# The low part of layer one's activations: made by VectorE in every step instead of by GpSimd in the first 75

## The chip, the cores and the metric

The kernel runs on one core of a Trainium2 chip. The metric is the time of one execution on the device in microseconds (us); lower is better. The core's engines run in parallel, each from its own queue, in order: PE (TensorE, matmuls), DVE (VectorE), ACT (ScalarE), POOL (GpSimd) and SP (SyncE, which here issues every DMA).

## The reference: Nystrom attention and two dense layers

```python
x = attn_out.transpose(...).reshape(2304, 512)      # Nystrom attention, 4 batches of 8 heads
h = x @ w_in                                        # layer one: 512 -> 2048
g = h * (1 / (1 + exp(-h)))
x = g @ w_out                                       # 2048 -> 512
h = x @ w_in2                                       # layer two, the same sizes
out = (h * tanh(log1p(exp(h)))) @ w_out2
```

All arrays are float32. The activation of layer one, g, is what the change touches.

## The kernel before, in words

Every product that must be exact is computed from split operands: a value x is kept as a high part (x rounded to the matmul's format) and a low part (x minus the high part), and a product is three matmuls, high times high, high times low and low times high (`mm3`, line 639 in the profile).

The program has three stretches. A prologue (to about 180 us) computes the attention of batches 0 and 1, converts the first layer's weights and does the first two blocks of layer one; its order on all engines is written out by a planner with costs. Then comes the loop this change is in: 96 steps `t`, each for one block of 288 tokens and one of 16 slices of the hidden layer. At the end (from about 470 us) layer two runs, in an order written by hand.

A step of the loop does the following. PE computes `h(t)` with six matmuls into one of two PSUM banks (`bank((4, 6)[t % 2])`), so the bank of step t is used again by step t+2. `silu2` then makes the activation in a chain of four instructions, each on the result of the one before: ACT takes the tanh (L698), DVE multiplies (L699; this is the last reader of the PSUM bank), ACT casts the result to the high part (L700), and one engine subtracts to get the low part (L701). PE then consumes both parts in the twelve matmuls of `y(t)`, which are issued two steps later (`LAG = 2`: `emit_y(t - LAG)`). The second of the twelve already needs the low part.

Other work is dealt out between the steps:

- `advance` issues the attention of batches 2 and 3: softmax pieces on POOL (L501, L509, L526), many small DVE instructions, and the Newton iterations, where PE (L441) and DVE (L445, L453) wait for each other in turn.
- `cv2` converts the weights of layer two. Each of its 32 pieces is loaded into one of three buffers by a DMA, clamped by POOL (L621), scaled twice by ACT (L623, L624) and put together by DVE (L626, L630).
- `u_all` makes the next batch's left operands.

In the first 75 steps (`t < AHEAD`) no order is prescribed: the framework orders each engine's instructions itself, by when its own model finds them ready, with earlier program text first. So instructions that stand side by side in the text (L626 and L630) can lie apart in the trace. From step 75 on, the order on ACT, DVE, PE and POOL is that of the program text (`manual_schedule`).

Of the kernel before, what the change touches and what calls it, by code (L numbers as in the profile page):

```python
# [25 lines left out]
AHEAD = 75  # L26
# [65 lines left out]
def nystrom_moe_kernel(ctx, tc, q, k, v, w1i, w1o, w2i, w2o, out):  # L92
# [10 lines left out]
    act, dve, pool, pe, sp = nc.scalar, nc.vector, nc.gpsimd, nc.tensor, nc.sync  # L103
# [38 lines left out]
    def bank(i, name):  # L142
        return ps.tile([P, 512], F32, tag=f"b{i}", name=name)
# [438 lines left out]
    def u_all(b, jq):  # L582
        for _ in u_steps(b, (2 * jq, 2 * jq + 1)):
            pass
# [86 lines left out]
    def h1_matmuls(hb, b, j, hf):  # L671
        uh, ul = uq[b, j // 4][:, 0], uq[b, j // 4][:, 1]
        sl = slice(hf * HB, (hf + 1) * HB)
        for g in range(2):
            wh, wl = uh[:, g, j % 4], ul[:, g, j % 4]
            xh, xl = ath[b][:, g, sl], atl[b][:, g, sl]
            mm3(hb[:, :HB], [(wh, xh), (wh, xl), (wl, xh)], g == 0, g == 1)
# [16 lines left out]
    def silu2(hb, gh, gl, name, eng=dve):  # L694

        th = mp.tile([P, HB], F32, tag="th", name="th" + name)
        g2 = mp.tile([P, HB], F32, tag="g2", name="g2" + name)
        tanhs.append(act.activation(th, hb[:, :HB], AF.Tanh, scale=0.5))  # L698
        dve.scalar_tensor_tensor(g2, th, 1.0, hb[:, :HB], op0=ALU.add, op1=ALU.mult)  # L699
        act.copy(gh, g2)  # L700
        eng.tensor_tensor(gl, g2, gh.bitcast(F32), op=ALU.subtract)  # L701
# [32 lines left out]
    def advance(n=1.0):  # L734
        credit[0] += n
        while credit[0] >= 1:
            credit[0] -= 1
            while bg:
                try:
                    next(bg[0])  # L740
                    break
                except StopIteration:
                    bg.pop(0)
# [9 lines left out]
    def attn_batch(b):  # L753
        if b == 2:
            yield Step((), [("wt", 1, 1), ("ath", 1, 1)] + [("ci", j) for j in OWN])
        for g in range(2):
            units[b, g] = new_unit(b, g)
            yield from whole_unit(units[b, g], True)
            if g == 1:
                yield from attn_newton(batches[b][g])  # L760
# [158 lines left out]
    gt = {}  # L919
# [21 lines left out]
    def open_second():  # L941
        rgt.close()
        late["pool"] = ctx.enter_context(tc.tile_pool(name="p2", bufs=1, side="right"))
# [78 lines left out]
    def left_steps(n):  # L1022

        if n >= NP:
            yield from left_loads(n)
            return
        f = Left(n)
        yield
        f.sums("s1", "s2", "s4")
        f.parts(1, 6)  # L1030
        yield
        f.sums("s3")
        f.parts(2, 7)
        yield
        f.parts(5, 4)
        yield
        f.parts(3)
        yield
# [36 lines left out]
    def out_weights(js, tile_of):  # L1075

        raws = []
        for n, j in enumerate(js):
            raw = tile_of(n)
            if is64:  # L1080
                sp.dma_start(raw, w2c[NF + j])
            else:
                sp.dma_start(raw.rearrange("p (a n) -> p a n", a=1), wout_src(w2o, j))
            raws.append(raw)
        yield
        for j, raw in zip(js, raws):
            hi, lo = wout_high(2, j), half(2, j)
            split(raw, hi, lo, pool)
            wout2[j] = (hi, lo)
            yield  # L1090

    def gtiles(t, n):
        gt_ = wp.tile([P, 2, n], F32R, tag=f"gt{t % 3}", name=f"g{t}_{n}")
        return gt_[:, 0], gt_[:, 1]

    def emit_y(t):
        i, j = steps1[t]
        if j == 0:
            ybank[i] = [bank(m, f"y{i}_{m}") for m in range(ND)]
        y_matmuls(ybank[i], wout[j], *gt.pop(("a", t)), j == 0, j == NF - 1)  # L1100
        if j == NF - 1:
            y_out(ybank[i], i)
# [3 lines left out]
    for t in range(len(steps)):  # L1106
        i, j = steps[t]
        b, hf = i // 2, i % 2
        if hf == 1 and b + 1 < B and j == SHIFT + 1:
            while bg:  # L1110
                advance()
            if b + 2 < B:
                bg.append(attn_batch(b + 2))
        if t == AHEAD:
            for _ in cv2:
                pass
            open_second()
            wx = [wp.tile([P, 768], F32, tag=f"wc{c}", name=f"x0_{c}") for c in (4, 5, 6)]
            xx = [xp.tile([P, 768], F32, tag=t, name=f"x0_{t}") for t in ("ath0", "atl0")]
            xx += [lambda: wp.tile([P, 768], F32, tag="wl7", name="x0_wl")]  # L1120
            r0, l0 = Right(0, wx + xx), Left(0, dve)
            ls, wsteps = [], []

            def raw_pair(j):
                tile_ = wp.tile([P, 2, 512], F32, tag="wc7", name=f"wr{j}")
                wsteps.append(out_weights((j, j + 1), lambda n: tile_[:, n]))
                next(wsteps[-1])

            plan = {
                2: lambda: r0.sum(1),  # L1130
                3: lambda: (r0.sum(3), r0.put(1, dve)),
                4: lambda: (r0.sum(2), l0.sums("s1")),
                5: lambda: (l0.sums("s2"), r0.put(6, dve)),
                6: lambda: (l0.sums("s4"), r0.put(7, dve), raw_pair(0)),
                7: lambda: (l0.sums("s3"), r0.put(2, dve)),
                8: lambda: r0.sum(4),
                9: lambda: (l0.parts(1), r0.put(5, dve), next(wsteps[0])),
                10: lambda: (l0.parts(6), r0.put(4, dve), next(wsteps[0])),
                11: lambda: (l0.parts(2), r0.put(3, dve)),
                12: lambda: (l0.parts(7, 5), raw_pair(2)),  # L1140
                13: lambda: (l0.parts(4, 3), ls.append(Left(1))),
                14: lambda: next(wsteps[1]),
                15: lambda: next(wsteps[1]),
                16: lambda: (ls[0].sums("s1", "s2"), ls.append(left_steps(2)), next(ls[1])),
                17: lambda: (ls[0].sums("s4"), ls[0].parts(1, 6)),
                18: lambda: (ls[0].sums("s3"), ls[0].parts(2, 5)),
                19: lambda: ls[0].parts(7, 4),
                20: lambda: ls[0].parts(3),
            }
            turn = ExitStack()  # L1150
            turn.enter_context(tc.manual_schedule(engines={act.engine, dve.engine, pe.engine, pool.engine}))
        hb = bank((4, 6)[t % 2], f"h{t}")
        h1_matmuls(hb, b, j, hf)
        gt["a", t] = gtiles(t, HB)
        silu2(hb, *gt["a", t], f"{t}", pool if t < AHEAD else dve)
        lin = NF * hf + j - NF - 1 - SHIFT
        if lin >= 0 and lin % 4 == 0 and b + 1 < B:
            u_all(b + 1, lin // 4)
        lin += 2 * NF
        if b > 1 and lin < NF and lin % 4 == 0:  # L1160
            u_all(b, lin // 4)
        advance(RB)
        if t < AHEAD:
            while cvn[0] < min(34, (18 * (t - 11) // 52 if t < 64 else t - 45)):
                cvn[0] += 1
                next(cv2, None)
        if t >= LAG:
            emit_y(t - LAG)
        if t >= AHEAD and t - AHEAD in plan:
            plan[t - AHEAD]()  # L1170
        advance(RB)
# [234 lines left out]
```

## Time and profile before

| | us |
|---|---|
| median of three runs | 850.02 (849.99 to 851.71) |
| the profiled execution | 849.09 |
| its span, first to last instruction | 847.3 |
| PE busy over the span | 816.8 (96%) |
| DVE busy | 518.3 (61%) |
| ACT busy | 349.4 (41%) |
| POOL busy | 213.8 (25%) |

The spans of the instructions are from the hardware profiler. A wait is the idle time of an engine in front of an instruction, put down to what released it. "PEld" is the weight load that runs ahead of each matmul. A clock of 1.00 is TensorE's full level, 0.50 its half level.

### The profile page before, as it was taken

The page shows a single profiled execution, that of the slowest core. Times are in us where ns is not written, and L with a number is a line of the kernel's source. Part 1 is how long each engine was busy: PE and PEld are TensorE (multiplying, and loading weights), DVE is VectorE, ACT ScalarE, POOL GpSimd, SP SyncE. Part 2 cuts the span into 40 slices and gives each one's busy share as a digit, 9 for nine tenths or more (in the row PEclk, how much of TensorE's full clock was granted, in tenths as well). Part 3 has the DMA queues.
Part 4 walks back from the last instruction along what each step waited for, and adds up shares of the span by engine and source line. Part 5 has one row for each costly group of instructions (what it writes and reads, how often), then busy time and mean ns, then how long its engine had stood idle before and what let it go on. Part 6 is the DMA issues. An engine that isn't in the chain of part 4 may idle for free.

```text
span 847.3 us, 14581 instructions
## 1 busy us (share of the span) xinstructions
PE 816.8 (96%) x5350; PEld 718.0 (85%) x5350; DVE 518.3 (61%) x1067; ACT 349.4 (41%) x787; POOL 213.8 (25%) x256
## 2 busy tenths in 40 slices
PE   8789999999999998899999999999999999999998
PEld 6656776769999797899999989999999999899996
DVE  4878877687575868773386765656533456534433
ACT  4657655355344646664456543424211124211111
POOL 1311333015342536543113654512000002000000
PEclk9999999999999999999999999999999999999999
DMA  8735474335337455752216854445733334533301
GB/s 243 205 103 153 149 231 140 70 97 156 87 84 196 121 151 206 240 180 85 70 43 220 299 204 174 158 165 163 233 103 130 119 112 137 183 115 112 125 1 74
DMA packets 109175, 123.64 MB, mean 146 GB/s; under 512 B 54064, under 2 KB 82224, under 8 KB 109104
## 3 DMA queue, kind: packets, MB, share of 16 engines
q1 hardware_dynamic: 109104, 122.72, 46.4%
q8 instruction: 42, 0.69, 0.4%
q14 instruction: 29, 0.24, 0.1%
HBM read 90.18 MB, written 32.51 MB: 145 GB/s over the span
## 4 chain that ended last, share of the span: by engine, by line
PE 77%; DVE 8%; issue 4%; POOL 4%; ACT 3%; DMA 2%; SPq 2%; POOLq 0%; DVEq 0%; ACTq 0%
PE o L1226 23%; PE y L639 14%; PE px L1241 12%; PE py L1241 9%; PE h L639 7%; PE ha L669 4%; PE ya L872 3%; PE u L556 2%; SPq L216 1%; POOL g L701 1%; PE nw L441 1%; POOL rawt L621 1%; DMA rawo<-in_moe_w_out_dram 1%; PE cv L390 1%; DMA k<-in_k_dram 1%
## 5 line engine op out<-in xcount | busy, mean ns | idle before, releaser
L639 PE MATMUL y<-g,wh 128*128 128x288 f32 x768 | 162.3, 302 | 6.1 <-POOL g L701 3.9
L1226 PE MATMUL o<-wh,gm 128*128 128x512 f32 x576 | 166.3, 392 | 0.0
L639 PEld LDWEIGHTS y<-g,wh 128*128 128x128 f32 x768 | 124.8, 190 | 12.4 <-POOL g L701 5.3
L1226 PEld LDWEIGHTS o<-wh,gm 128*128 128x128 f32 x576 | 107.1, 188 | 16.5
L639 PE MATMUL y<-g,wl 128*128 128x288 f32 x384 | 115.0, 299 | 0.0
L1241 PE MATMUL px<-r,le 128*128 128x384 f32 x564 | 114.2, 338 | 0.1
L1241 PEld LDWEIGHTS px<-r,le 128*128 128x128 f32 x564 | 101.1, 188 | 7.6 <-ACT u L1344 0.6
L701 POOL TENSOR_TENSOR g<-g,g 128x288 fp32r<-128x288 f32 x75 | 64.7, 863 | 148.0 <-ACT g L700 114.5
L639 PE MATMUL h<-ath,uw 128*128 128x288 f32 x384 | 94.8, 301 | 1.9 <-DVE g L699 1.9
L1265 DVE TENSOR_TENSOR u<-u,py 128x384 f32<-128x384 f32 x47 | 26.0, 554 | 103.0 <-PE py L1241 102.9
L1241 PE MATMUL py<-r,le 128*128 128x384 f32 x420 | 85.2, 338 | 0.0
L1226 PE MATMUL o<-wl,gm 128*128 128x512 f32 x288 | 84.8, 389 | 0.0
L699 DVE SCALAR_TENSOR_TENSOR g<-th,h 128x288 f32<-128x288 f32 x96 | 43.1, 450 | 52.1 <-ACT th L698 47.9
L1241 PEld LDWEIGHTS py<-r,le 128*128 128x128 f32 x420 | 74.6, 188 | 0.3 <-DVE u L1265 0.3
L639 PEld LDWEIGHTS y<-g,wl 128*128 128x128 f32 x384 | 73.0, 190 | 0.4 <-issue 0.4
L639 PEld LDWEIGHTS h<-ath,uw 128*128 128x128 f32 x384 | 67.6, 190 | 5.8 <-issue 2.8
L872 PE MATMUL ya<-gs,wl 128*128 128x288 f32 x256 | 68.3, 412 | 1.1 <-DVE yo L726 0.9
L700 ACT CAST g<-g 128x288 fp32r<-128x288 f32 x96 | 41.4, 432 | 57.6 <-DVE g L699 57.4
L1226 PEld LDWEIGHTS o<-wl,gm 128*128 128x128 f32 x288 | 54.1, 188 | 11.4
L698 ACT ACTIVATE th<-h 128x288 f32<-128x288 f32 x96 | 39.3, 409 | 54.3 <-PE h L639 53.2
L872 PEld LDWEIGHTS ya<-gs,wl 128*128 128x128 f32 x256 | 46.6, 190 | 15.5 <-issue 2.6
L639 PE MATMUL h<-atl,uw 128*128 128x288 f32 x192 | 57.1, 297 | 0.0
(218 smaller groups left out, 1252.2 us busy)
## 6 DMA issues: line engine op xcount, KB each, us to landing
le<-lsc SPq DMA_DIRECT2D x48, 512.0 KB, 3.3
lsc<-le SPq DMA_DIRECT2D x24, 512.0 KB, 2.9
rawi<-in_moe_w_in_dram SPq DMA_DIRECT2D x16, 512.0 KB, 4.8
rawo<-in_moe_w_out_dram SPq DMA_DIRECT2D x16, 512.0 KB, 3.6
rawt<-in_moe_w_in_dram SPq DMA_DIRECT2D x16, 512.0 KB, 4.5
w2c<-ct SPq DMA_DIRECT2D x32, 256.0 KB, 2.4
rawt<-in_moe_w_out_dram SPq DMA_DIRECT2D x16, 512.0 KB, 4.0
v<-in_v_dram SPq DMA_DIRECT2D x32, 144.0 KB, 3.3
```

Source lines behind the costliest of these rows:

```text
L216: sp.dma_start(t[:, h2] if apart else t[:, :, h2, :], src[b, heads[h2]].rearrange("(p c) d -> p c d", c=NC))
L556: pe.matmul(ub[g][32 * h : 32 * h + 32, 2 * P * n : 2 * P * n + 2 * P].rearrange("a (j f) -> a j f", j=2), units[b, g]["wt"][sl, h], wcp[j ...
L639: pe.matmul(o, a, b_, start=first and i == 0, stop=last and i == n - 1)
L669: pe.matmul(hb[:, :HB], uq[0, j // 4][:, g, j % 4], ath[0][:, g, hf * HB : (hf + 1) * HB], start=g == 0, stop=g == 1)
L698: tanhs.append(act.activation(th, hb[:, :HB], AF.Tanh, scale=0.5))
L699: dve.scalar_tensor_tensor(g2, th, 1.0, hb[:, :HB], op0=ALU.add, op1=ALU.mult)
L700: act.copy(gh, g2)
L701: eng.tensor_tensor(gl, g2, gh.bitcast(F32), op=ALU.subtract)
L872: pe.matmul(yb[hf, m][:, :HB], wof[j][:, m * P : (m + 1) * P], gst[j // 4][:, j % 4, hf], start=j == 0, stop=j == NF - 1,)
L1226: pe.matmul(obank[ch], g[:, c * P : (c + 1) * P], w, start=p == 0 and ch not in seen, stop=end)
L1241: pe.matmul(o, x[:, dt], y[:, dt], start=first and m == 0, stop=m == 5, skip_group_check=True)
L1265: dve.tensor_tensor(o, a, b_, op=ALU.add)
```

## The change

```diff
         hb = bank((4, 6)[t % 2], f"h{t}")
         h1_matmuls(hb, b, j, hf)
         gt["a", t] = gtiles(t, HB)
-        silu2(hb, *gt["a", t], f"{t}", pool if t < AHEAD else dve)
+        silu2(hb, *gt["a", t], f"{t}", dve)
```

The last argument is the engine of L701, `eng.tensor_tensor(gl, g2, gh.bitcast(F32), op=ALU.subtract)`: 128 partitions by 288 elements, two inputs in SBUF. Of the 96 instructions, 75 change engine. Nothing else in the program text changes.

## Rows read from the trace of the kernel before

**Rows 1.** Windows: us; busy us (and instructions) per engine; clock; DMA share; GB/s.
```profile
184.00:416.00 232.00, 220.97 (x1850) 204.88 (x1847) 152.34 (x336) 119.15 (x281) 103.06 (x116) 0.99 0.50 147
180.00:200.00 20.00, 18.03 (x129) 15.46 (x129) 15.87 (x32) 11.48 (x30) 8.54 (x10) 1.00 0.61 168
200.00:220.00 20.00, 19.90 (x163) 19.48 (x163) 17.09 (x39) 10.59 (x24) 10.45 (x12) 1.00 0.47 107
...
280.00:300.00 20.00, 17.91 (x147) 16.49 (x144) 17.54 (x38) 13.40 (x33) 12.13 (x13) 0.93 0.47 138
...
320.00:340.00 20.00, 16.59 (x117) 14.61 (x116) 17.45 (x35) 12.30 (x30) 13.73 (x14) 1.00 0.58 201
...
360.00:380.00 20.00, 20.00 (x177) 18.97 (x176) 15.27 (x28) 12.49 (x29) 10.45 (x12) 1.00 0.57 192
```

**Rows 2.** Waits of PE, 184 to 416 us: waiter, releaser, total us, times, longest.
```profile
PEld y L639 <- POOL g L701: 5.3, 6, 2.3
PE nw L441 <- DVE rv L453: 2.3, 1, 2.3
```

**Rows 3.** Line 701's instructions: duration ns min/median/max, first and last start.
```profile
L701 POOL TENSOR_TENSOR g<-g,g x75: 791/807/1355, 185.5 to 413.8; 128x288 fp32r<-128x288 f32 x75
...
L701 DVE TENSOR_TENSOR g<-g,g x21: 457/459/611, 416.2 to 465.3; 128x288 fp32r<-128x288 f32 x21
```

**Rows 4.** Waits of DVE in the last 21 steps, columns as in rows 2.
```profile
DVE g L701 <- ACT g L700: 10.5, 21, 0.6
```

**Rows 5.** Timeline, 293 to 297 us: start, length, engine, line, operation [idle before].
```profile
293.23 0.43 ACT L700 CAST g<-g 128x288 fp32r<-128x288 f32 x1 [1.28 <-DVE g L699]
...
294.37 0.68 DVE L626 SCALAR_TENSOR_TENSOR rawt<-rawt 128x512 uint32<-128x512 uint32 x1
...
295.08 0.64 POOL L621 TENSOR_SCALAR rawt<-rawt 128x512 f32<-128x512 f32 x1 [2.80 <-DMA rawt<-in_moe_w_in_dram]
295.67 0.80 POOL L701 TENSOR_TENSOR g<-g,g 128x288 fp32r<-128x288 f32 x1
...
296.13 0.46 DVE L699 SCALAR_TENSOR_TENSOR g<-th,h 128x288 f32<-128x288 f32 x1 [1.07 <-ACT th L698]
...
296.52 0.40 PE L639 MATMUL y<-g,wh 128*128 128x288 f32 x1 [2.09 <-POOL g L701]
```

**Rows 6.** Windows of 2 us around two stalls of PE, columns as in rows 1.
```profile
296.00:298.00 2.00, 1.48 (x8) 1.48 (x9) 1.82 (x4) 1.71 (x5) 1.33 (x2) 0.79 0.48 151
298.00:300.00 2.00, 2.00 (x11) 1.95 (x10) 1.00 (x3) 0.75 (x2) 1.24 (x2) 0.50 0.00 0
300.00:302.00 2.00, 2.00 (x38) 1.31 (x38) 1.75 (x5) 0.56 (x2) 0.00 (x0) 0.86 0.12 19
...
334.00:336.00 2.00, 0.80 (x6) 0.54 (x5) 2.00 (x4) 0.33 (x1) 1.25 (x1) 1.00 0.85 250
```

**Rows 7.** Timeline, 350 to 354 us, columns as in rows 5.
```profile
351.15 1.08 POOL L621 TENSOR_SCALAR rawt<-rawt 128x512 f32<-128x512 f32 x1
...
352.95 0.69 DVE L626 SCALAR_TENSOR_TENSOR rawt<-rawt 128x512 uint32<-128x512 uint32 x1 [0.88 <-ACT rawt L623]
...
353.90 0.69 PE L441 MATMUL nw<-rv,rb 128*128 128x96 f32 x4 [2.30 <-DVE rv L453]
```

**Rows 8.** DVE, two lines of the weight conversion: durations, columns as in rows 3.
```profile
L626 DVE SCALAR_TENSOR_TENSOR rawt<-rawt x29: 670/694/1518, 201.5 to 375.5; 128x512 uint32<-128x512 uint32 x29
...
L630 DVE SCALAR_TENSOR_TENSOR ct<-rawt x32: 636/686/1643, 187.7 to 376.2; 128x512 uint32<-128x512 uint32 x32
```

**Rows 9.** Groups by line, 184 to 416 us: busy us, mean ns | idle before.
```profile
L701 POOL TENSOR_TENSOR g<-g,g 128x288 fp32r<-128x288 f32 x75 | 64.7, 863 | 148.0 <-ACT g L700 114.5 <-PE y L639 28.1 <-issue 4.4
...
L630 DVE SCALAR_TENSOR_TENSOR ct<-rawt 128x512 uint32<-128x512 uint32 x32 | 27.5, 861 | 0.2
L626 DVE SCALAR_TENSOR_TENSOR rawt<-rawt 128x512 uint32<-128x512 uint32 x29 | 23.6, 814 | 11.5 <-ACT rawt L623 11.2
```

**Rows 10.** Timeline near 206 us, columns as in rows 5.
```profile
205.56 0.44 DVE L699 SCALAR_TENSOR_TENSOR g<-th,h 128x288 f32<-128x288 f32 x1
...
206.41 0.29 PE L639 MATMUL h<-ath,uw 128*128 128x288 f32 x1
```

## The prediction

> **What bounds the kernel now.** I read the windows first, to see which engine is short in the stretch of the change. From 184 to 416 us, where the 75 subtractions lie on POOL, PE is busy 220.97 of 232 us at a clock of 0.99, DVE 152.34, ACT 119.15 and POOL 103.06 [rows 1]. So PE is the bound of the stretch, and only two things can move its end: PE's idle 11 us, and the little time at the lower clock. Off PE, the 20 us windows differ: DVE is busy 15.3 to 17.5 us in five of them (180, 200, 280, 320 and 360), and PE loses time in three of these. DVE's share over the whole stretch (66%) therefore says little; the five windows decide.
>
> Next come PE's waits. Weight loads of `y` waited for POOL's subtraction six times, 5.3 us in all, the longest 2.3; a single wait of the Newton matmuls for DVE cost 2.3 [rows 2]. Last I read the timelines at the longest of each kind, for what stood in the queue ahead of the late instruction [rows 5, 7].
>
> **What moves, and its cost.** POOL loses 75 instructions with a median of 807 ns, 64.7 us in all [rows 3, 9]. DVE gains 75, and the last 21 steps show the same shape there at a median of 459 ns [rows 3]: 75 x 0.459 = 34.4 us. No DMA, matmul or ACT instruction is added or taken away. What this is worth is worked out at the places where PE stands still.
>
> *First term, the six waits for POOL.* At the longest, the cast ended at 293.23 + 0.43 = 293.66. POOL's in-order queue had a weight clamp ahead of the subtraction, and the clamp waited for its DMA until 295.08; the subtraction ran at 295.67 and PE went on at 296.52 [rows 5]. On DVE no clamp stands ahead: DVE ran continuously up to and through L626 at 294.37, so the subtraction fits between two of its instructions and ends near 294.3, just when PE wanted it. PE stood from about 294.27 to 296.52, 2.25 us. But a second chain is late here: the DVE multiply that frees an h bank starts only at 296.13 and ends at 296.59, because ACT's tanh was late. PE, with eleven y matmuls at about 0.134 us and 0.5 us of transposes, would want that bank at about 296.3. So about 0.4 of the 2.25 comes back as a new wait. I take 1.8 saved. The other five waits sum to 5.3 - 2.3 = 3.0, 0.6 each. There the subtraction is 0.807 - 0.459 = 0.35 shorter, and it escapes POOL's queue but waits for whatever DVE has in hand (half of some 0.7 us, by the medians of [rows 8]). The bounds are nothing saved and 3.0; I take two thirds, 2.0. First term: 3.8 us.
>
> *Second term, the clock.* After the 2.25 us stall the granted clock drops: 0.79, 0.50 and 0.86 in the three windows from 296 to 302 [rows 6]. At the half level (1.2 of 2.4 GHz) that is 0.84 + 2.0 + 0.56 = 3.4 us, and half of the work of that time, 1.7 us, is lost. A stall that leaves PE busy 0.80 of 2 us at 334 us went by at 1.00 [rows 6]. What remains of the stall at 294 is shorter than that, so I take 1.7, with nothing as the other end.
>
> *Third term, the clamp released from behind the subtraction.* At 351.15 a clamp ran directly behind a late subtraction in POOL's queue. The ACT scaling behind it made DVE wait 0.88 us in front of L626; L626 stood ahead of the Newton update L453 in DVE's queue, and PE waited 2.30 us for that [rows 7]. With no subtraction in POOL's queue the clamp goes when its data is there, and the 0.88 goes. Taken: 0.9; other end nothing, since DVE's own lateness is then what is late next.
>
> *Fourth term, what DVE gives back.* In the five dense windows DVE is idle 4.13 + 2.91 + 2.46 + 2.55 + 4.73 = 16.8 us of 100 [rows 1]. There are 75 subtractions in 232 us, so 6.5 a window: 32 x 0.459 = 14.7 us come into 16.8 us of idle. Something goes out again. L626 and L630 have medians of 694 and 686 ns but means of 814 and 861, with maxima of 1518 and 1643: (0.814 - 0.694) x 29 + (0.861 - 0.686) x 32 = 9.1 us lost, and in the timeline the long ones lie beside POOL instructions [rows 8, 9]. The subtractions are 64.7 of POOL's 103.06 us, 63%, so about 5.7 us of that loss should go with them. The load then just fits, but locally it will be late where a DVE multiply already frees its bank at the last moment: at 205.56 + 0.44 = 206.0, against PE's use of that bank at 206.41 [rows 10]. I charge one subtraction, 0.46 us, to the path in each of the five windows: 2.3 us. The bounds are nothing, and, if every added microsecond in the dense windows reached PE, 14.7.
>
> The Trainium skill (SBUF — State Buffer, section "SBUF: two separate sides") says that a DVE instruction with two SBUF inputs and a GpSimd instruction exclude each other from a shared port pair for the whole instruction. The trace agrees in size: L630's longest is 1.64 us against 0.69 [rows 8]. The rule speaks for the change where it frees L626 and L630, and against it since the subtraction itself has two SBUF inputs; the third rival weighs that.
>
> Sum: 3.8 + 1.7 + 0.9 - 2.3 = 4.1 us saved. The profiled execution took 849.09 us (its span 847.3 and 1.8 around it), so one like it should take 845.0. The median of the runs is 0.93 higher; I forecast 850.02 - 4.1 = 845.9 us. From step 75 on nothing changes, so the gain stays to the end.
>
> **Rivals.** *First: DVE held by the subtraction's own wait; slower.* In the last 21 steps DVE waits 10.5 / 21 = 0.50 us in front of each subtraction, since the cast takes that long and nothing else may pass [rows 4]. If the framework's order puts the subtraction straight behind the multiply in the first 75 too, a step costs DVE 0.46 + 0.50 = 0.96 us. In the five dense windows that is 32 x 0.96 = 30.7 us, against 16.8 of idle and 5.7 of relief: 8.2 us over, which PE waits for. In place of the fourth term's 2.3: 8.2 - 6.4 = 1.8 us slower, 851.8 us; windows of middling load add perhaps 1 or 2, so 853. It decides from a mean wait of (16.8 + 5.7 + 6.4) / 32 - 0.46 = 0.44 us on. For it: the chain of [rows 4] is the same. Against it: in the first 75 steps small DVE instructions and L626/L630 are there to go in between, and the framework orders by readiness.
>
> *Second: the gain is handed back.* The six waits go, but the multiplies and Newton updates come later by as much: fourteen of the 32 dense subtractions on the path, 14 x 0.46 = 6.4, cancel the three gains. 850.0 us. For it: PE's next waits are DVE's already [rows 2], and the order of 75 steps is drawn up afresh, so stalls can land elsewhere. Against it: 11 us of PE's idle is all there is, and DVE has 80 us of idle.
>
> *Third: the subtractions meet the rest of POOL's work.* POOL keeps 103.06 - 64.7 = 38.4 us in 41 instructions, 17% of the stretch [rows 1, 9]. Then 75 x 0.17 = 12 subtractions meet one and wait half of its 0.94 us: 5.6 us of DVE, which takes the place of the relief. If all of it reached PE: 5.6 - 4.1 = 1.5 slower, 851.5 us. Against it: the slowest subtraction on DVE so far took 611 ns where the median is 459 [rows 3].
>
> *Fourth: more comes free.* The stall of 2.3 us at the Newton step is also followed by the lower clock; if it shrinks enough, that clock loss and the rest of PE's idle go too: another 1.7 + 2, about 842 us.
>
> **How the numbers follow.** A measurement of this kernel can tell 0.2%, 1.7 us, from no change. The forecast's own range is 843 to 848 us, with a chance of 0.45; the fourth rival has 0.07, the second 0.20, the third 0.08, the first 0.20. Faster: 0.45 + 0.07 = 0.52. Within 0.2%: 0.20 + 0.08 = 0.28. Slower: 0.20. For 8 in 10 the range runs from 842 (half of the fourth rival left out) to 853 (half of the first left out).
>
> **What would show each step.** L701 stands with 96 on DVE at about 0.46 to 0.5 us, and no wait of PE for POOL's g is left (first term). The clock stays at 1.00 near 296 us (second). POOL's clamps no longer make ACT and DVE wait as long, and PE's longest Newton wait is under 2 us (third). The means of L626 and L630 fall towards 0.7 us, and PE's waits for DVE's L699 and L701 sum to 2 to 3 us (fourth). It would be wrong if DVE's idle in front of L701 comes to more than about 33 us (75 x 0.44), or if PE's waits for DVE grow by over 6 us.

## The result, and the profile after

The changed kernel takes 843.71 us (median of five runs, 841.7 to 845.28) against 850.02 for the kernel before: the ratio is 0.9911 with a 95% interval of 0.9892 to 0.9929, so 6 to 9 us are saved. A second comparison, on another chip, gave 0.9904 (0.9875 to 0.9932). The forecast was 845.9. Its direction and range hold; the gain is larger than the 4.1 us worked out, and it is made up in another way than the sum had it.

The profiled executions can be compared more sharply by stretches of the loop, each from the first h matmul of one step to that of another. Behind step 95 every profile here shows 380.5 us to the end of the last matmul, and step 0 starts anywhere between 179.7 and 186.9 us, so the loop itself is what carries the change. The second profile of the changed kernel says how far a stretch can be trusted: its loop is 1.2 us longer than the first one's. Differences under about 1.5 us are not read below.

| us | steps 0-11 | 11-33 | 33-58 | 58-75 | 75-95 | loop, 0-95 |
|---|---|---|---|---|---|---|
| before | 29.8 | 68.6 | 89.9 | 45.6 | 49.2 | 283.2 |
| changed | 28.1 | 68.6 | 83.3 | 45.7 | 49.2 | 274.9 |
| changed, second profile | 28.0 | 68.6 | 84.5 | 45.7 | 49.2 | 276.1 |

Of 8.3 us, 1.7 are gained in the first eleven steps and 6.6 in steps 33 to 58. The windows of the changed kernel answer to [rows 1], with the same columns (the loop lies about 4 us later at its start and 4 earlier at its end):

```profile
184.00:416.00 232.00, 224.64 (x1908) 208.06 (x1901) 179.96 (x420) 124.86 (x292) 39.51 (x41) 1.00 0.51 149
180.00:200.00 20.00, 18.76 (x157) 15.22 (x150) 18.20 (x38) 11.16 (x26) 3.95 (x3) 1.00 0.48 132
200.00:220.00 20.00, 20.00 (x165) 19.79 (x165) 19.33 (x51) 11.75 (x28) 3.47 (x4) 1.00 0.50 119
...
280.00:300.00 20.00, 20.00 (x173) 17.62 (x170) 18.80 (x43) 12.83 (x32) 6.09 (x6) 1.00 0.37 101
300.00:320.00 20.00, 17.63 (x163) 16.06 (x164) 15.62 (x41) 9.10 (x21) 1.78 (x3) 1.00 0.62 185
320.00:340.00 20.00, 18.47 (x138) 16.68 (x138) 18.36 (x42) 14.62 (x35) 8.83 (x9) 1.00 0.58 190
...
360.00:380.00 20.00, 19.98 (x197) 18.07 (x196) 17.18 (x35) 12.81 (x28) 3.74 (x5) 1.00 0.59 202
```

POOL falls from 103 to 40 us and DVE rises by 27.6, to 78% of the stretch and 91 to 97% of four dense windows; even so PE gains 3.7 us of busy time. PE's waits (180 to 412 us; waiter, releaser, total us, times, longest) answer to [rows 2]:

```profile
PE y L639 <- ACT g L700: 1.5, 1, 1.5
PE nw L441 <- DVE rv L453: 1.4, 1, 1.4
PE u L556 <- ACT ct L376: 1.3, 1, 1.3
PE nb L381 <- DVE uw L575: 1.1, 1, 1.1
PE h L639 <- DVE g L699: 0.7, 1, 0.7
PE nw L441 <- DVE rv L413: 0.6, 1, 0.6
PE c L323 <- DVE ta L488: 0.5, 1, 0.5
```

No wait for POOL is left, and each other one occurs once. The groups of the changed kernel on DVE answer to [rows 9] (busy us, mean ns | idle before), and behind them stand the wait that answers to [rows 4] and ACT's wait for the clamps:

```profile
L701 DVE TENSOR_TENSOR g<-g,g 128x288 fp32r<-128x288 f32 x75 | 36.8, 491 | 16.0 <-ACT g L700 15.6
...
L630 DVE SCALAR_TENSOR_TENSOR ct<-rawt 128x512 uint32<-128x512 uint32 x32 | 25.7, 803 | 0.0
L626 DVE SCALAR_TENSOR_TENSOR rawt<-rawt 128x512 uint32<-128x512 uint32 x30 | 20.7, 689 | 3.5 <-ACT rawt L623 3.1
```
```profile
DVE g L701 <- ACT g L700: 15.6, 30, 1.2
...
ACT rawt L623 <- POOL rawt L621: 2.7, 4, 1.8
```

In the kernel before (184 to 416 us) ACT's wait for the clamps was:

```profile
ACT rawt L623 <- POOL rawt L621: 13.4, 14, 1.6
```

DVE waits 15.6 / 75 = 0.21 us in front of a subtraction, not 0.50: the framework put other work in between. L626 and L630 fell by 125 and 58 ns each, together 3.6 + 1.9 = 5.5 us. L701 lost (0.491 - 0.459) x 75 = 2.4 us to what POOL still does: of the 74 subtractions that start on DVE between h of step 0 and h of step 75, the 17 that ran beside a POOL instruction took 631 ns in the mean, the other 57 took 450 and none of them more than 461.

### The profile page after: what moved, and what is told of

It reads as the page before. It is cut to its first block, busy times and chain, and to the rows that moved or that the text cites. A ratio compares the mean times of both kernels' runs of the same rounds, so it can differ in the third digit from the quotient of the medians.

```text
span 843.5 us, 14509 instructions
## 1 busy us (share of the span) xinstructions
PE 814.6 (97%) x5350; PEld 717.2 (85%) x5350; DVE 540.2 (64%) x1142; ACT 350.6 (42%) x787; POOL 150.8 (18%) x181
## 4 chain that ended last, share of the span: by engine, by line
PE 77%; DVE 10%; DMA 5%; ACT 3%; SPq 2%; issue 2%; POOL 1%; DVEq 0%; POOLq 0%; ACTq 0%
PE o L1226 23%; PE y L639 14%; PE px L1241 12%; PE py L1241 9%; PE h L639 7%; PE ha L669 4%; PE ya L872 3%; PE u L556 2%; DMA rawo<-in_moe_w_out_dram 2%; DMA q<-in_q_dram 1%; PE nw L441 1%; DMA rawt<-in_moe_w_in_dram 1%; DVE ct L630 1%; DVE wl L630 1%; SPq L205 1%
## 5 line engine op out<-in xcount | busy, mean ns | idle before, releaser
L639 PE MATMUL y<-g,wh 128*128 128x288 f32 x768 | 159.0, 299 | 2.5 <-ACT g L700 1.5
L639 PEld LDWEIGHTS y<-g,wh 128*128 128x128 f32 x768 | 123.2, 188 | 7.0 <-issue 2.5
L639 PE MATMUL y<-g,wl 128*128 128x288 f32 x384 | 113.9, 297 | 0.0
L639 PE MATMUL h<-ath,uw 128*128 128x288 f32 x384 | 93.8, 299 | 0.7 <-DVE g L699 0.7
L639 PEld LDWEIGHTS y<-g,wl 128*128 128x128 f32 x384 | 72.3, 188 | 0.8 <-issue 0.8
L639 PEld LDWEIGHTS h<-ath,uw 128*128 128x128 f32 x384 | 67.0, 188 | 4.3 <-issue 2.2
L701 DVE TENSOR_TENSOR g<-g,g 128x288 fp32r<-128x288 f32 x96 | 46.7, 487 | 26.5 <-ACT g L700 26.0
L700 ACT CAST g<-g 128x288 fp32r<-128x288 f32 x96 | 41.4, 432 | 53.3 <-DVE g L699 52.8
L699 DVE SCALAR_TENSOR_TENSOR g<-th,h 128x288 f32<-128x288 f32 x96 | 42.8, 447 | 27.1 <-ACT th L698 26.7
L639 PE MATMUL h<-atl,uw 128*128 128x288 f32 x192 | 56.9, 297 | 0.0
```

The lines of the kernel that those rows point to most:

```text
L639: pe.matmul(o, a, b_, start=first and i == 0, stop=last and i == n - 1)
```

## Experiments

Ratios are to the kernel before, in runs on the same chip, with 95% intervals. "Loop" is steps 0 to 95 as in the table above.

### Where the gain is made: steps on DVE

```diff
-        silu2(hb, *gt["a", t], f"{t}", dve)
+        silu2(hb, *gt["a", t], f"{t}", dve if t < 11 or 33 <= t < 58 or t >= AHEAD else pool)   # dense
+        silu2(hb, *gt["a", t], f"{t}", pool if t < 11 or 33 <= t < 58 else dve)                 # light
```

> The subtraction is on DVE in 36 of the first 75 steps, those of the dense windows (steps 0 to 10 and 33 to 57), and on POOL in the other 39. My theory (the gain is made where PE stood still, and those places lie in the dense windows): as the changed kernel, 843 to 845 us, and the loop from step 0 to step 95 about 275 us as there. The rival (the gain is the shorter subtraction, 0.35 us in every step): about half of it, 847 us.

> The complement: DVE in the 39 light steps (11 to 32, 58 to 74), POOL in the 36 dense ones. My theory: no gain, 849 to 851 us, and the loop about 283 us as before the change. The rival (a shorter subtraction in every step): about half of the gain, 847 us. A second rival (the gain is that the framework orders the loop anew, whatever is moved): a change of some us in either direction with stalls in other places.

Measured: the dense version has a ratio of 0.9935 (0.9912 to 0.9957) and a loop of 276.5 us; the light one 1.0003 (0.9981 to 1.0026) and 282.5. In the dense version steps 0 to 11 take 28.0 us and 33 to 58 take 84.3. So 36 of the 75 moves make nearly all of the gain, and the other 39 none that can be told (0.6 us of loop): it is not a shorter subtraction in every step, and not the fresh order as such.

### What POOL's load costs, and what DVE's costs

```diff
+        if t < AHEAD:
+            dm = mp.tile([P, HB], F32R, tag="dm", bufs=1, name=f"dm{t}")
+            pool.tensor_tensor(dm, extra[0], extra[1].bitcast(F32), op=ALU.subtract)
```

(`extra` holds g2 and gh of the step, the two inputs of L701. The second kernel has `dve.tensor_tensor` in the same place.)

> The changed kernel, with a copy of each of the 75 subtractions added on POOL whose result nobody reads. POOL is as full as before and the weight clamps stand behind the copies again, but PE waits for no POOL result. My theory (the place in POOL's queue): PE's waits for POOL's g and the clock loss after the longest of them do not come back; the clamps are held again, and DVE carries the subtractions beside a full POOL. So about half of the gain stays: 846 to 848 us. The rival (what counts is POOL's load itself, through the ports it shares with DVE): the whole gain goes and DVE's added work comes on top, 850 to 853 us. If POOL's load counts for nothing: 843 to 844.5 us.

> The changed kernel, with a copy of each of the 75 subtractions added on DVE too, whose result nobody reads: DVE gets another 34 us. DVE was idle 8.1 us in the five dense windows of the changed kernel and would get 32 x 0.46 = 14.7 there. My theory (DVE is now almost the bound of the dense windows): 6 to 9 us slower than the changed kernel, 850 to 853 us. The rival (DVE has room, PE alone is the bound): within 1.5 us of the changed kernel, 843 to 845 us.

Measured with the copies on POOL: ratio 1.0091 (1.0056 to 1.0126), loop 288.2 us. My theory fell here: PE waits for no POOL result in this kernel, and still it is slower than the one before. The rival named the mechanism and was short on the size. Measured with the copies on DVE: 0.9991 (0.9965 to 1.0016), loop 280.5 us. So a POOL copy costs the loop 288.2 - 274.9 = 13.3 us, and a DVE copy 5.6. In total the two add up to the change, 274.9 + 13.3 - 5.6 = 282.6, where the kernel before has 283.2. That is chance, for by stretches they do not. In steps 33 to 58 the POOL copies cost 8.3 us (91.6 against 83.3) and the DVE copies nothing (81.9), so the same sum would give 93.0 us there, where the kernel before takes 89.9. The DVE copies lose 2.2 us in steps 0 to 11 and 4.2 in steps 58 to 75, where they pushed five of the 19 weight conversions that the changed kernel makes in steps 33 to 58. So my theory for the DVE copies had the size nearly right, and the place, the dense windows, in part wrong. POOL's copies also run beside a DVE that subtracts, which POOL's subtractions before the change did not. The groups of the kernel with POOL copies (180 to 425 us):

```profile
L1161 POOL TENSOR_TENSOR dm<-g,g 128x288 fp32r<-128x288 f32 x75 | 73.6, 981 | 136.9 <-ACT g L700 136.8
...
L701 DVE TENSOR_TENSOR g<-g,g 128x288 fp32r<-128x288 f32 x76 | 45.1, 595 | 16.3 <-ACT g L700 15.9
...
L630 DVE SCALAR_TENSOR_TENSOR ct<-rawt 128x512 uint32<-128x512 uint32 x32 | 29.7, 930 | 0.0
...
L626 DVE SCALAR_TENSOR_TENSOR rawt<-rawt 128x512 uint32<-128x512 uint32 x30 | 24.6, 820 | 3.5 <-ACT rawt L623 3.2
```

Against the changed kernel L701 lost 104 ns, L630 127 and L626 131: 7.9 + 4.1 + 3.9 = 15.9 us of DVE time. ACT's wait for the clamps is also back, at 13.5 us. Either could be the cause. On PE's side 10.9 of the 13.3 us can be seen: PE stands 9.2 us longer from step 0 to 75, and one drop of the clock takes 1.7.

### Ports or queue

```diff
+        if t < AHEAD:
+            for _ in range(3):
+                pool.memset(extra[0], 0.0)      # g2 of this step
```

> The changed kernel with three memsets of 128x288 added on POOL in each of the first 75 steps (they overwrite a tile that all its readers are done with). POOL is held for about as long as by the subtraction, but by instructions that only write. The copies on POOL made the loop (first h matmul of step 0 to first h matmul of step 95) 288.2 us long, against 274.9 in the changed kernel. If that came from POOL and DVE blocking each other where both read SBUF: the memsets cost little, loop 275 to 278 us, ratio to before 0.991 to 0.995. If it came from the clamps and softmax pieces standing behind something in POOL's queue: as with the copies, loop 285 to 289 us, ratio 1.005 to 1.010.

Measured: ratio 0.9931 (0.9903 to 0.9959), loop 277.9 us.

```profile
L1161 POOL MEMSET g<- 128x288 f32 x225 | 76.1, 339 | 129.8 <-DVE g L701 121.5
L701 DVE TENSOR_TENSOR g<-g,g 128x288 fp32r<-128x288 f32 x81 | 41.0, 508 | 19.1 <-ACT g L700 17.4 <-PE h L639 1.4
...
L630 DVE SCALAR_TENSOR_TENSOR ct<-rawt 128x512 uint32<-128x512 uint32 x32 | 23.5, 736 | 0.0
L626 DVE SCALAR_TENSOR_TENSOR rawt<-rawt 128x512 uint32<-128x512 uint32 x30 | 21.6, 720 | 4.6 <-ACT rawt L623 4.3
```

POOL is held for longer than by the copies (76.1 us against 73.6), yet DVE's instructions stay near the changed kernel's means, and of the 13.3 us only 3.0 are left, 1.7 of them one drop of the clock. So about 10 us came with POOL instructions that read SBUF, the smaller part with POOL's queue being held. Two reserves. Three short memsets let a clamp in between, and ACT's wait for clamps was 5.8 us here, not 13.5; a part of the 10 may therefore be the queue's. And each memset waits for its step's subtraction, where a copy starts with it: only 21 of 74 subtractions ran beside a POOL instruction, 73 with the copies. L626 and L630 do not have this second reserve: 52 of 62 ran beside POOL and took 738 ns in the mean, with the copies 45 of 62 took 952. The Trainium skill (SBUF — State Buffer, section "SBUF: two separate sides") says that a DVE instruction with two SBUF inputs is shut out only by a GpSimd instruction that reads SBUF, a condition that the prediction left out. By that rule the memsets would cost no port time, and the means of 508 and 595 ns agree.

### The clock after the long wait

```diff
         h1_matmuls(hb, b, j, hf)
+        if t == 38:
+            fill(hb, 12)
```

> The kernel before, with twelve matmuls of 128x128 (about 1.3 us) put between h of step 38 and y of step 36, so that PE works through more than half of its longest wait for POOL's g. The framework's order is the same up to there and shifts a little behind it, so only the stretch up to h of step 40 is compared: 124.6 us from step 0's first h in the kernel before. My second term (the wait takes the clock down for 3.4 us): the clock stays at 1.00 from 296 to 302 us, and the stretch is 1.7 us shorter, 122.9 us. The rival (the clock falls whatever fills the wait, or its loss is hidden): 124.6 us or more.

Measured: the stretch to h of step 40 takes 124.2 us, 0.36 less than before. The two profiles of the changed kernel differ by 0.85 us in this stretch, so no gain is shown, and the 1.7 us expected did not come. The windows show the clock at full and what became of the time:

```profile
296.00:298.00 2.00, 2.00 (x20) 2.00 (x19) 2.00 (x4) 1.76 (x4) 1.98 (x2) 1.00 0.45 73
298.00:300.00 2.00, 2.00 (x18) 2.00 (x17) 2.00 (x3) 1.13 (x3) 1.14 (x2) 1.00 0.84 202
...
304.00:306.00 2.00, 0.96 (x8) 0.73 (x7) 2.00 (x4) 1.33 (x3) 0.14 (x1) 1.00 0.46 74
```

DVE is busy throughout (2.00 of 2 us), and PE stands at 304 instead of working slowly at 298: there it waits 1.04 us for DVE's L575. Two things keep this from pricing the clock in the kernel before. The twelve added matmuls show as 24 in the trace and took 2.6 us, so the second matmul of y came 3.70 us behind h of step 38, where it came 3.27 behind it after the stall; the fill itself cost 0.43. And DVE's order changed: L308 (0.93 us) and L630 (0.68) ran ahead of L575, which in the kernel before came behind it, and there DVE was idle for half of the window from 298 to 300 us [rows 6]. What the full clock alone is worth at this place is not shown.

### DVE in text order

```diff
         if t == AHEAD:
+            early.close()
...
+        if t == 0:
+            early = ExitStack()
+            early.enter_context(tc.manual_schedule(engines={dve.engine}))
```

> The changed kernel, with DVE's order in the first 75 steps that of the program text, so that the subtraction stands directly behind the multiply and waits for the cast at the head of DVE's queue, as in the last 21 steps. The prediction's first rival: about 0.5 us of wait in front of each subtraction, and with more than 0.44 the gain is gone: loop 285 us or more, 852 us or more where the kernel before takes 850. The alternative (such waits fall into DVE's idle time): loop 275 to 279 us, still faster than before.

Measured: ratio 1.0355 (1.0308 to 1.0402), loop 310.9 us. DVE's wait (180 to 425 us):

```profile
DVE g L701 <- ACT g L700: 43.7, 72, 1.7
```

The wait is 0.61 us for each subtraction, above the break-even of 0.44, and the kernel is much slower. The size says less than it seems: the rest of DVE's work is in text order too, and conversions that did not fit come behind step 75 (steps 75 to 95 take 62.2 us, not 49.2). The rival's danger was real; the framework's order avoids it.

### Spreading the weight conversions

```diff
-        pool.tensor_scalar(hf, hf, TOP, -TOP, op0=ALU.min, op1=ALU.max)
+        clamp = pool.tensor_scalar(hf, hf, TOP, -TOP, op0=ALU.min, op1=ALU.max)
+        if pace:
+            after(clamp, tanhs[-1], "spread")
...
-            while cvn[0] < min(34, (18 * (t - 11) // 52 if t < 64 else t - 45)):
+            pace[:] = [1]
+            while cvn[0] < min(34, 34 * (t + 1) // 72):
```

(`after` holds a clamp back until the tanh of its step. The second version leaves the first nine conversions as they fall and deals the other 23 out over steps 33 to 74.)

> The changed kernel, with the 32 weight conversions spread evenly over the 75 steps (each clamp is held back to the step it is dealt to; so far the framework ran them early, and the last one was done by step 60). If what is left of PE's waits comes from DVE being full in the dense windows: 2 to 5 us faster than the changed kernel, loop 270 to 273 us, ratio to before 0.986 to 0.989. If it comes from the attention's own chains: no change, loop 274 to 276 us.

> The changed kernel, with the weight conversions left as they fall up to the ninth, and the other 23 held back: 12 dealt to steps 33 to 57, 11 to steps 58 to 74 (in the changed kernel 19 fall into steps 33 to 57 and the last is done at step 62). The even spread made steps 33 to 58 3.1 us shorter and steps 11 to 33 3.3 us longer. If DVE's load decides steps 33 to 58 and steps 58 to 74 have room for eleven conversions: steps 0 to 33 as in the changed kernel (96.7 us), 33 to 58 about 80 us instead of 83.3, 58 to 75 under 47; loop 271 to 273 us, ratio to the changed kernel 0.995 to 0.998. If the conversions only take their waits along with them: loop 274 to 277 us.

> The changed kernel once more, beside the one before on the same chip: the loop 274 to 276 us against 282 to 284, 0.989 to 0.993 of the time before. It is there so that the later conversions are compared with it on one chip.

Measured: spread evenly, the loop is 275.4 us (0.9900, 0.9865 to 0.9934), like the changed kernel. Steps 33 to 58 fell to 80.3 us and steps 11 to 33 rose to 72.0. Held back only behind step 33, the loop is 279.6 (0.9957, 0.9931 to 0.9983): 33 to 58 take 83.0 and 58 to 75 take 50.8 instead of 45.7. The changed kernel again: 276.1, ratio 0.9904. Both spreads miss: the conversions take their time along. In the second one the trace shows what steps 58 to 75 lost: the 5.1 us are one wait of PE for ACT, 3.4 us, and the drop of the clock behind it, 1.7. (In this kernel L624, L639, L700 and L724 stand as L626, L641, L703 and L727.) The wait of PE, from steps 58 to 75, and ACT's queue ahead of it:

```profile
PE y L641 <- ACT yo L727: 3.4, 1, 3.4
```
```profile
382.67 0.68 ACT L626 ACTIVATE rawt<-rawt 128x512 uint32<-128x512 uint16 x1 [2.22 <-DMA rawt<-in_moe_w_out_dram]
383.25 0.41 ACT L703 CAST g<-g 128x288 fp32r<-128x288 f32 x1
```

A weight scaling stood at the head of ACT's queue for 2.22 us until its DMA had landed. The cast behind it, whose input DVE had finished at 380.93, stood with it, and PE waited for ACT from 383.50 on. So the wait began in ACT's queue and not on DVE. What made the DMA late was not followed.

### More of POOL's work on DVE

```diff
-        pool.tensor_scalar(hf, hf, TOP, -TOP, op0=ALU.min, op1=ALU.max)
+        (dve if in_loop else pool).tensor_scalar(hf, hf, TOP, -TOP, op0=ALU.min, op1=ALU.max)   # clamps
-        pool.tensor_tensor(ta, ta, mx[:, 0]...)      # likewise L509 and L526
+        (dve if b > 1 else pool).tensor_tensor(ta, ta, mx[:, 0]...)                             # softmax
```

> The changed kernel, with the loop's weight clamps (L621, 23 us on POOL) on DVE as well. By the copies, POOL's time cost the loop 13.3 / 73.6 = 0.18 us per us, and DVE's 5.6 / 39.3 = 0.14. If these rates carry over: 0.18 x 23 = 4.2 saved, and 29 clamps of about 0.5 us on DVE (half of the 0.69 that two inputs of that size take, plus a fixed part) cost 0.14 x 14.5 = 2.1; loop 272 to 274 us, 0.985 to 0.989 of the time before. If DVE is full now and the clamps come at the wrong places: loop 277 us or more, 0.992 or more.

> The changed kernel, with the softmax pieces of batches 2 and 3 (L501, L509, L526: twelve instructions, 16.5 us on POOL) on DVE as well, where a 576-element instruction takes about 0.75 us. By the same rates: 0.18 x 16.5 = 3.0 saved, 0.14 x 9 = 1.3 lost; loop 272.5 to 274.5 us, 0.986 to 0.989 of the time before. If DVE is full now: they lie in the dense windows, so all 9 us could come through; loop 278 us or more, 0.994 or more.

Measured: with the clamps, ratio 0.9884 (0.9853 to 0.9915), loop 275.3 us, a miss: steps 33 to 58 gained 2.4 us (80.9), and 58 to 75 lost 3.6 (49.3), of which a wait of PE for ACT's cast is 1.9 and a drop of the clock 1.7. With the softmax pieces, 0.9856 (0.9827 to 0.9885), 841.4 us, and a loop of 272.1, a little better than the rates had it; steps 33 to 58 take 79.7. Its DVE groups (180 to 412 us):

```profile
L701 DVE TENSOR_TENSOR g<-g,g 128x288 fp32r<-128x288 f32 x78 | 36.9, 475 | 12.8 <-ACT g L700 12.7
...
L526 DVE TENSOR_TENSOR atl<-at,ath 128x576 fp32r<-128x576 f32 x4 | 3.0, 754 | 0.0
L509 DVE TENSOR_TENSOR ta<-ta,mx 128x576 f32<-128x576 f32 x4 | 3.0, 745 | 0.1
```

This version beats both kernels by its loop. Its interval overlaps that of the changed kernel measured again, so the step from one to the other is shown by the profiles (272.1 against 274.9 and 276.1), not by the run times.

## Why the prediction came out as it did

**The bound.** Right: the dense windows decide [rows 1], as the dense and light versions show, and PE's standstills are the currency. Those standstills, before and after, account for the gain. In the kernel before, PE's waits from 180 to 412 us, beside the Newton wait of 2.3 [rows 2], are:

```profile
PE y L639 <- POOL g L701: 3.9, 5, 2.1
PE h L639 <- DVE g L699: 1.9, 2, 1.2
PE y L639 <- ACT yo L724: 1.1, 1, 1.1
PE cv L390 <- ACT ct L376: 0.8, 1, 0.8
PE nw L441 <- DVE rv L413: 0.7, 1, 0.7
PE c L323 <- DVE ta L488: 0.5, 1, 0.5
```

Set against the list of the changed kernel above, with the clock's loss as half of the time at the half level:

| us | before | changed | saved | in the sum |
|---|---|---|---|---|
| waits for POOL's subtraction (first term) | 3.9 | 0 | 3.9 | 3.8 |
| the clock (second) | 3.4 | 0 | 3.4 | 1.7 |
| Newton wait for L453 (third) | 2.3 | 1.4 | 0.9 | 0.9 |
| all other waits (fourth) | 5.0 | 5.7 | -0.7 | -2.3 |
| together | 14.6 | 7.1 | 7.5 | 4.1 |

That is 7.5 of the 8.3 us. The sum fell short by 1.7 of clock and by 1.6 in the fourth term. From 320 to 366 us the kernel before had PE waits of 6.3 us and a clock loss; the changed one has 2.9 us in the same steps:

```profile
PE nw L441 <- DVE rv L453: 2.3, 1, 2.3
PE h L639 <- DVE g L699: 1.2, 1, 1.2
PE y L639 <- ACT yo L724: 1.1, 1, 1.1
PE y L639 <- POOL g L701: 1.0, 2, 0.8
PE nw L441 <- DVE rv L413: 0.7, 1, 0.7
```

(kernel before, 320 to 366 us, waits of PE; only 1.0 of the 6.3 are waits for POOL's result). The clock loss there followed the Newton wait; in the kernel before:

```profile
354.00:356.00 2.00, 2.00 (x13) 2.00 (x14) 1.43 (x4) 1.32 (x4) 1.25 (x2) 0.80 0.77 259
356.00:358.00 2.00, 2.00 (x10) 2.00 (x10) 1.38 (x3) 1.85 (x4) 0.84 (x2) 0.50 0.87 255
358.00:360.00 2.00, 2.00 (x15) 2.00 (x14) 1.03 (x3) 0.84 (x2) 1.71 (x3) 0.85 0.40 155
```

That is 0.8 + 2.0 + 0.6 = 3.4 us at the half level and 1.7 us lost. The changed kernel stays at 1.00 there. So the waits' 3.4 and the clock's 1.7 us are 5.1 of the 5.9 gained from step 41 to 58.

**First term (3.8).** The six waits went, as forecast, and as waits they were worth what the sum had. The close agreement (3.9 against 3.8) is luck: the sum counted 5.3 us of waiting weight loads [rows 2] and gave part of them back. Steps 0 to 11 gave 1.7 us. At the longest wait PE did not wait for L701, but met two other waits a few steps on, at 301.85 and 306.31 us:

```profile
301.85 1.09 PE L556 MATMUL u<-wc,wt 64*32 64x256 f32 x30 [1.31 <-ACT ct L376]
306.31 0.43 PE L381 MATMUL nb<-bc,blk 128*128 128x64 f32 x2 [1.06 <-DVE uw L575]
```

From step 36 to 41 only 1.0 us remained of the 1.8 + 1.7 that the first two terms had put there.

**Second term (1.7).** Half of it. The clock stayed at full near 296, as forecast, but of the stall and its clock loss, 3.8 us together, 2.4 came back as the two waits above. The filled stall points the same way, in a DVE order of its own. The sum had at nothing the second clock loss, after the Newton wait, which stood under the fourth rival.

**Third term (0.9).** Right in size: the Newton wait fell from 2.3 to 1.4 us, and DVE's wait in front of L626 from 11.2 us in all [rows 9] to 3.1. That the clock would then stay up was left to a rival with a chance of 0.07.

**Fourth term (2.3 lost).** This is the step that failed. It charged DVE's added load to the path with 2.3 us, with 14.7 as the worst, and booked the freed ports only as a relief that makes the load fit. The relief was measured well (5.5 us on L626 and L630 against 5.7 forecast). The loss was not: PE's other waits rose by 0.7 us. Those for L699 fell from 1.9 to 0.7, where I had expected them to grow; the new ones are ACT's (1.5 and 1.3) and DVE's L575 (1.1), 3.9 us in all. The copies point to the reason: POOL's load costs the loop more than the same work on DVE does, 13.3 us against 5.6, and in steps 33 to 58 8.3 against nothing. The memsets tie most of the 13.3 to POOL's reads. How a DVE with 15.9 us more to do comes to lose that much of the loop, where 75 added copies of its own (39.3 us busy) lose only 5.6, is not shown step by step.

**Rivals.** The first did not occur: 0.21 us of wait for each subtraction, not 0.50; the kernel in text order shows that it would have been slower. The third was 2.4 us of DVE instead of 5.6. The fourth came half true, with the second clock loss gone. The kernel came out between the forecast and it.

## What to carry to other kernels

Before work goes to the idle engine, price what it does to the busy one: here POOL's reading instructions, added as copies, cost the loop more than twice what the same copies cost on DVE, and the stretched DVE instructions gave it away. Price a stall with the waits that come next behind it: at the longest stall 3.8 us went and 2.4 came back. List every drop of the clock with the stall ahead of it: here two drops of 1.7 us each went, and the sum had one. Judge such a move by the dense windows alone; the 39 moves in the light ones were worth nothing that could be told.

## What was not expected of the hardware

The spread from run to run of this kernel sits in its prologue: in fourteen profiled executions step 0 started between 179.7 and 186.9 us, while the part behind step 95 took 380.5 us every time, and two profiles of the same kernel differ by 1.2 us in the loop. The clock goes with it: before step 0 the two profiles that start at 179.7 and 180.1 have no time at the half level, the three that start at 186.8 to 186.9 have 13.7 us of it, 6.8 us lost. And a wait of 2.3 us at the Newton step was followed by 3.4 us at the half clock level, one of 1.4 us in the same place by none:

```profile
350.00:352.00 2.00, 1.22 (x10) 1.22 (x11) 2.00 (x5) 1.92 (x5) 0.66 (x1) 1.00 0.33 120
352.00:354.00 2.00, 2.00 (x18) 2.00 (x17) 2.00 (x6) 1.20 (x4) 0.00 (x0) 1.00 0.88 274
354.00:356.00 2.00, 2.00 (x18) 2.00 (x17) 1.54 (x4) 1.48 (x4) 0.91 (x1) 1.00 0.90 327
```

(changed kernel, windows of 2 us behind the Newton wait; seventh column of figures: the granted clock).
